# Token ring, squares' sums, held-back scores and the softmax's order in a fused attention and feed-forward kernel

## The chip, the cores and the metric

The kernel runs on one core of one Trainium2 chip. The metric is the device time of one execution in microseconds (us). Five engines work side by side, each with a queue of its own that it goes through in order: TensorE (PE in the profile, with its weight loads as PEld), VectorE (DVE), ScalarE (ACT), GpSimd (POOL) and SyncE (SP), which issues the transfers (DMA). They wait for one another by semaphores.

## What is computed

q, k and v are 6016 x 256. Attention goes over channels: the scores are a 256 x 256 matrix, summed over all tokens, of columns divided by their norms. Two feed-forward layers follow, with weights of 256 x 2048 and 2048 x 256 each.

```python
qn = q / (np.linalg.norm(q, axis=1, keepdims=True) + 1e-06)
kn = k / (np.linalg.norm(k, axis=1, keepdims=True) + 1e-06)
s = kn.transpose(0, 2, 1) @ qn / tau
s = s - s.max(-1, keepdims=True)
a = np.exp(s)
a /= a.sum(-1, keepdims=True) + 1e-09
x = v @ a
h = x @ w_in1;  x = (h * np.clip(h + 3.0, 0.0, 6.0) / 6.0) @ w_out1
h = x @ w_in2;  x = np.maximum(h, 0.0) ** 2 @ w_out2
```

## The kernel before

The whole program is written in one hand-made order (`manual_schedule`): the order of the calls in the code is the order on each engine's queue.

**Scores.** The tokens come in NT = 47 tiles of 128, q and k side by side, 256 KB a tile. GROUPS says how many tiles one transfer carries: one, then 23 times two. The transfers go through SP's queue into a ring of eight buffers (the tags wo0 to wo7); a transfer waits until TensorE has read the buffer's former tiles. For each tile ScalarE squares its 512 columns into a PSUM bank (`squares`, sq), VectorE adds the squares to one of two sums (`sums[t % 2]`), and TensorE adds to both halves of the scores (`score`: `s_ps[0]`, in the order's rows s_113, and `s_ps[1]`, s_114), each a float32 matmul of two passes. Of the last DEFER = 10 tiles the second half is held back (`late`). Ahead of the first tile come six fillers, matmuls on ones (`keep_busy`) that compute nothing.

**w_in1.** The weights arrive as 64-bit floats in units of 512 KB, which ScalarE and VectorE turn into pairs of float32r numbers, high and low, in several steps (`unit`, `from_float64`). Unit 0 is asked for with group 12 and converted while the scores run. Unit 1 (raw11l) is asked for behind the last group of q and k and converted behind the last tile.

**Softmax.** The norms' sums over the partitions are 8 matmuls with ones (`nrm`), one for each of the two sums and four blocks of columns. Then six of the held-back scores run while VectorE and ScalarE take the root, polish it and invert it. `rq_ps` spreads the inverse norms of q over the partitions; ScalarE copies it (L428). For each half, VectorE multiplies scores by both norms (L435), takes the row maximum (L439), and ScalarE takes the exponential (L442). TensorE transposes the result (`et_ps`), ScalarE and VectorE cut it into high and low parts (eth, etl). Fillers stand between.

**M and the first feed-forward layer.** M = et x w_in1 (256 x 2048) takes the place of v @ a @ w_in1. Its quarters c4 = 0 to 3 are made in two banks each (`mps`: mp_0, mp_1), which ScalarE and VectorE turn into weights (`m1_out`: wa_0h, wa_0l, a_0); `m1_keep` copies both banks to SBUF (m_01) for sums of M's blocks, which GpSimd and others make later. Then the steps of the loop run: a product of v's first 1024 tokens with M's blocks (h_n_f, `product` and `whole_product`), relu on ScalarE (`relu0`, L661), the gate on VectorE (`gate0`, L666), the cut into high (ScalarE, gs) and low (VectorE), and the accumulation with w_out1 (`second_both`, acc_0_n_d, LAG = 2 products behind). M's next quarter comes behind the product h_0_3.

## Time and profile before

| | us |
|---|---|
| median of 3 runs | 1039.83 |
| lowest and highest | 1038.69, 1040.44 |
| the profiled execution | 1040.8 |
| its span | 1039.0 |
| TensorE busy in the span | 1031.2 (99%) |
| VectorE, ScalarE, GpSimd busy | 855.5, 664.2, 30.9 |

The span runs from the first to the last instruction that the profile shows. Its stages are: start and scores up to 42 us, softmax up to 55.6 us, M's first quarter and the first steps up to 73.8 us, then the two feed-forward layers. A busy share says nothing on who waits for whom; for that one reads the stage, the idle time in front of an instruction, and what ended it.

### The profile page before, as it was taken

To read this page: it belongs to the slowest core of one execution; us is meant where nothing else is said; L and a number is where in the kernel's file an instruction comes from. 1 tells how busy PE (TensorE), PEld (TensorE's weight loads), DVE (VectorE), ACT (ScalarE), POOL (GpSimd) and SP (SyncE) were. 2 spreads that over 40 slices of the span, in tenths; PEclk is the share of its full clock that TensorE was granted. 3 is DMA by queue.
4 is the path that set the end of the run, shared out by engine and by line. 5 is a ranking of instruction groups with operands and counts; after the bars stand their busy time and mean duration, and the time that the engine had idled before them with its cause. 6 is when DMAs were issued, how large, how long until landed. Compare 5 with 4: busy or idle time off the path is not lost.

```text
span 1039.0 us, 12962 instructions
## 1 busy us (share of the span) xinstructions
PE 1031.2 (99%) x4630; PEld 867.5 (83%) x4630; DVE 855.5 (82%) x1429; ACT 664.2 (64%) x1200; POOL 30.9 (3%) x33
## 2 busy tenths in 40 slices
PE   9999999999999999999999999999999999999998
PEld 8878888888888888888998888888888888888997
DVE  6889978889989889888988688688688688778765
ACT  6788877788787878878766455445445455445443
POOL 0012240000000000000000000000000000000000
PEclk9999999999999999999999999999999999999999
DMA  9911203003403403302755002002001000200100
GB/s 363 355 29 53 83 14 130 1 1 130 145 1 116 157 1 117 131 23 103 261 184 188 1 1 81 0 1 81 1 1 47 36 1 6 71 1 1 41 1 36
DMA packets 25936, 77.64 MB, mean 75 GB/s; under 512 B 2832, under 2 KB 4880, under 8 KB 25872
## 3 DMA queue, kind: packets, MB, share of 16 engines
q1 hardware_dynamic: 25872, 76.82, 21.1%
q8 instruction: 36, 0.59, 0.2%
q14 instruction: 28, 0.23, 0.1%
HBM read 52.95 MB, written 23.86 MB: 74 GB/s over the span
## 4 chain that ended last, share of the span: by engine, by line
PE 96%; DVE 1%; ACT 1%; DMA 1%; issue 0%; SPq 0%
PE acc L323 15%; PE acc L322 15%; PE acc L321 15%; PE y L322 8%; PE y L323 8%; PE y L321 8%; PE q L323 4%; PE q L321 4%; PE q L322 4%; PE acc L689 4%; PE h L311 3%; PE s L300 3%; PE x L323 2%; PE x L321 2%; PE x L322 2%; PE mp L311 1%
## 5 line engine op out<-in xcount | busy, mean ns | idle before, releaser
L126 DVE TENSOR_TENSOR gs<-g,gs 128x512 fp32r<-128x512 f32 (+1 forms) x384 | 263.9, 687 | 60.2 <-ACT gs L841 48.1
L323 PE MATMUL acc<-gs,wo 128*128 128x512 f32 (+1 forms) x708 | 273.0, 386 | 0.1
L322 PE MATMUL acc<-gs,wo 128*128 128x512 f32 (+1 forms) x708 | 272.9, 385 | 0.0
L321 PE MATMUL acc<-gs,wo 128*128 128x512 f32 (+1 forms) x708 | 272.9, 385 | 0.0
L841 ACT CAST gs<-g 128x512 fp32r<-128x512 f32 (+1 forms) x352 | 208.1, 613 | 27.5 <-DVE g L832 18.9
L323 PEld LDWEIGHTS acc<-gs,wo 128*128 128x128 f32 x708 | 133.0, 188 | 25.2 <-DVE gs L126 0.5
L322 PEld LDWEIGHTS acc<-gs,wo 128*128 128x128 f32 x708 | 133.0, 188 | 24.8
L321 PEld LDWEIGHTS acc<-gs,wo 128*128 128x128 f32 x708 | 133.0, 188 | 24.4
L814 ACT COPY se<-y 128x512 f32<-128x512 f32 (+1 forms) x88 | 50.8, 577 | 124.1 <-PE y L323 124.0
L818 DVE TENSOR_TENSOR h<-q,se 128x512 f32<-128x512 f32 (+1 forms) x88 | 59.7, 678 | 65.5 <-ACT se L814 65.0
L814 ACT COPY su<-y 128x512 f32<-128x512 f32 (+1 forms) x88 | 50.8, 577 | 87.7 <-PE y L323 76.7
L837 DVE SCALAR_TENSOR_TENSOR g<-h 128x512 f32<-128x512 f32 (+1 forms) x144 | 97.1, 675 | 0.0
L824 ACT ACTIVATE r<-h,three 128x512 f32<-128x512 f32 (+1 forms) x120 | 85.6, 713 | 7.8 <-DVE h L818 7.5
L832 DVE SCALAR_TENSOR_TENSOR g<-r,h 128x512 f32<-128x512 f32 (+1 forms) x120 | 80.9, 674 | 3.9 <-ACT r L824 3.8
L826 ACT ACTIVATE r<-y 128x512 f32<-128x512 f32 (+1 forms) x48 | 28.3, 590 | 62.5 <-PE y L323 62.5
L818 DVE TENSOR_TENSOR h<-q,su 128x512 f32<-128x512 f32 (+1 forms) x88 | 59.5, 676 | 1.5
L818 DVE TENSOR_TENSOR h<-x,sa 128x512 f32<-128x512 f32 (+1 forms) x88 | 59.3, 674 | 0.0
L814 ACT COPY sa<-y 128x512 f32<-128x512 f32 (+1 forms) x88 | 50.7, 576 | 7.5 <-PE y L323 1.5
L837 DVE SCALAR_TENSOR_TENSOR g<-y,r 128x512 f32<-128x512 f32 (+1 forms) x48 | 32.7, 681 | 23.3 <-ACT r L826 22.7
L689 PE MATMUL acc<-gs,wo 128*128 128x512 f32 x180 | 45.3, 391 | 0.0
L300 PE MATMUL s<-qk 128*128 128x256 f32 x188 | 42.2, 385 | 0.9 <-DMA qk<-in_qk 0.9
L300 PEld LDWEIGHTS s<-qk 128*128 128x128 f32 x188 | 36.2, 194 | 6.1 <-DMA qk<-in_qk 1.3
(247 smaller groups left out, 1802.2 us busy)
## 6 DMA issues: line engine op xcount, KB each, us to landing
qk<-in_qk SPq DMA_DIRECT2D x23, 512.0 KB, 7.2
wo<-in_w_out SPq DMA_DIRECT2D x16, 512.0 KB, 5.6
wi<-in_w_in SPq DMA_DIRECT2D x10, 512.0 KB, 5.5
...
```

The lines of the kernel that those rows point to most:

```text
L126: eng.tensor_tensor(out=lo, in0=x, in1=f32(hi), op=ALU.subtract)
L300: nc.tensor.matmul(s_ps[i], lhsT=x[:, C + i * P:C + (i + 1) * P], rhs=x[:, :C], start=(t == 0), stop=(t == NT - 1))
L321: nc.tensor.matmul(ps, lhsT=ah, rhs=bh, start=first, stop=False, skip_group_check=more)
L322: nc.tensor.matmul(ps, lhsT=al, rhs=bh, start=False, stop=False, skip_group_check=more)
L323: nc.tensor.matmul(ps, lhsT=ah, rhs=bl, start=False, stop=last, skip_group_check=more)
L689: nc.tensor.matmul(acc[0, 0, n, d], lhsT=wo1[u][:, i, at + d * P:at + (d + 1) * P], rhs=gs[k], start=f == 0 and (i, k) == (0, 0), stop=f = ...
L814: nc.scalar.copy(s[tag], s["y"])
L818: nc.vector.tensor_tensor(out=s[which], in0=s[ps], in1=s[tag], op=ALU.add)
L824: nc.scalar.activation(s["r" + which], h, AF.Relu, bias=three)
L832: nc.vector.scalar_tensor_tensor(out=g, in0=s["r" + which], scalar=6.0, in1=h, op0=ALU.min, op1=ALU.mult)
L837: nc.vector.scalar_tensor_tensor(out=g, in0=h, scalar=0.0, in1=r, op0=ALU.max, op1=ALU.mult)
L841: nc.scalar.copy(gs[which][0], s["g" + which])
```

## The change

- *Transfers.* The first five tiles come one by one. The ring has twelve buffers, four of them (b4 to b7) the converter's tags. Units 0 and 1 of w_in1 are asked for with groups 8 and 14 and converted inside the loop, one step behind each of twelve tiles (CONVERT). tau's transfer moves from group 20 to group 10.
- *Sums.* There are three. The first tile of each is squared right into its sum, so the memsets go. Ten tiles (BY_POOL) go to the third, whose nine adds GpSimd makes from a square in SBUF; behind tile 42 VectorE adds it to the second. The later tiles all go to the first. The norms of the second sum are taken ahead of the last tile but one's scores, those of the first behind the last tile.
- *Scores held back.* 14, of which 6, 3 and 5 are issued (LATE).
- *Softmax.* The table of the exponential is loaded behind the root. One instruction, `tensor_tensor_reduce`, multiplies and takes the maximum; a small one negates it. The first half reads `rq_ps` in place; ScalarE has multiplied its scores by k's norms. The fillers of this stage go (seven), and there are seven at the start.
- *M and the first steps.* mp_0 and mp_1 are each made in one run (`m1_first`). The tokens' high parts are cut ahead of the second half's softmax. The first two products are made high parts first (`first_products`). h_1_0 and h_1_1 lie in the accumulators' banks. `m1_keep` copies mp_0 in step 1 and mp_1 in step 2 instead of ahead of the first product.

```diff
-GROUPS = [1] + [2] * 23
-DEFER = 10
-LATE_AT = 6
+GROUPS = [1] * 5 + [2] * 21
+RING = ("b4", "b5", "wo0", "wo1", "wo2", "wo3", "b6", "b7", "wo4", "wo5", "wo6", "wo7")
+DEFER = 14
+LATE = (6, 3, 5)
...
-BUSY = (6, 2, 2, 3)
+BUSY = 7
...
-EARLY = 12
-TAU_AT = 20
-EARLY_AT = {15: (0, 1), 16: (2,), 18: (3, 4)}
+EARLY = {8: 0, 14: 1}
+TAU_AT = 10
+CONVERT = {
+    15: (0, 0), 16: (0, 1), 17: (0, 2), 18: (0, 3), 19: (0, 4, 0), 20: (0, 4, 1),
+    27: (1, 0), 28: (1, 1), 29: (1, 2), 30: (1, 3), 31: (1, 4, 0), 32: (1, 4, 1),
+}
+BY_POOL = (4, 7, 10, 13, 22, 24, 26, 33, 35, 37)
+JOIN_AT = 42
+FIRST_SUM_AT = 45
...
     def squares(t, x):
-        sq = bank([P, 2 * C], f"sq{t}")
+        at, eng = (2, nc.gpsimd) if t in BY_POOL else (0 if t > JOIN_AT else t % 2, nc.vector)
+        if at not in begun:
+            begun.add(at)
+            nc.scalar.activation(sums[at], x, AF.Square)
+            return
+        if at == 2:
+            sq = hpool.tile([P, 2 * C], F32, tag="r", name=f"sq{t}")
+        else:
+            sq = bank([P, 2 * C], f"sq{t}")
         nc.scalar.activation(sq, x, AF.Square)
-        nc.vector.tensor_tensor(out=sums[t % 2], in0=sq, in1=sums[t % 2], op=ALU.add)
+        eng.tensor_tensor(out=sums[at], in0=sq, in1=sums[at], op=ALU.add)
...
+                if t == JOIN_AT:
+                    nc.vector.tensor_tensor(out=sums[1], in0=sums[1], in1=sums[2], op=ALU.add)
+                if t == FIRST_SUM_AT:
+                    nrm = ps_acc.tile([P, 8], F32, tag="acc", name="nrm")
+                    norms(4, 1)
                 score(t, x, 0)
...
+        norms(0, 0)
+        late_scores(LATE[0])
+        first = small(4)
+        nc.vector.tensor_copy(first, nrm[:, 4:8])
...
+        late_scores(LATE[1])
+        s0k = small(C)
+        nc.scalar.activation(s0k, s_ps[0], AF.Copy, scale=rnorm[:, 2:3])
...
-            nc.vector.scalar_tensor_tensor(
-                out=s, in0=s_ps[i], scalar=rnorm[:, 2 + i:3 + i], in1=rq, op0=ALU.mult, op1=ALU.mult
+            mx, low = small(1), small(1)
+            a, b, scale = (s0k, rq_ps, 1.0) if i == 0 else (s_ps[1], rq, rnorm[:, 3:4])
+            nc.vector.tensor_tensor_reduce(
+                out=s, in0=a, in1=b, scale=scale, scalar=-3.0e38, op0=ALU.mult, op1=ALU.max, accum_out=mx
             )
-            mx = small(1)
-            nc.vector.tensor_reduce(out=mx, in_=s, axis=AX.X, op=ALU.max, negate=True)
+            nc.vector.tensor_scalar(out=low, in0=mx, scalar1=-1.0, scalar2=None, op0=ALU.mult)
...
+        e0 = softmax(0)
+        nc.scalar.copy(rq, rq_ps)
+        loaded[0][2]()
+        loaded[0][3]()
+        transposed(0, *e0)
+        rest(0, *e0)
+        row_sums(0, *e0)
+        late_scores(LATE[2])
+        for k in range(KC):
             for n in range(2):
...
+                first_tokens(k, n, 0)
+        for n in range(2):
+            first_tokens(0, n, 1)
         e1 = softmax(1)
...
+        m1_first(0)
+        transposed(1, *e1)
+        row_sums(1, *e1)
+        for n in range(2):
+            first_tokens(1, n, 1)
+        rest(1, *e1)
+        m1_high(0, 0)
+        m1_first(1)
+        m1_low(0, 0)
+        m1_high(0, 1)
+        m1_low(0, 1)
...
-        m1_keep(0)
...
+                if at in (2, 3):
+                    hs[at] = ps_acc.tile([P, WMAX], F32, tag="acc", name=name)[:, :w0]
+                else:
+                    hs[at] = bank([P, WMAX], name)[:, :w0]
...
+            if a in (1, 2):
+                m1_keep(0, (a - 1,))
```

SP's queue near the end of the tokens, before (raw11l is unit 1 of w_in1, v the first tokens of v):

```order
L338 DMA qk_379<-in_qk 128x1024 [waits DMAHW5_49,PE_49,Activation_49]
L346 DMA tau_sb<-in_tau 128x1 [waits DMAHW6_49]
L338 DMA qk_392<-in_qk 128x1024 [waits DMAHW7_49,PE_49,Activation_49]
L338 DMA qk_402<-in_qk 128x1024 [waits DMAHW0_49,PE_49,Activation_49]
L338 DMA qk_412<-in_qk 128x1024 [waits DMAHW1_49,PE_49,Activation_49]
L184 DMA raw11l<-in_w_in 128x1024 [waits DMAHW2_49]
L380 DMA v_0_425<-in_vt 128x1024 [waits DMAHW3_49]
L380 DMA v_1_426<-in_vt 128x1024 [waits DMAHW4_49]
```

And now, with the last group of tokens at the second piece's head:

```order
L361 DMA qk_285<-in_qk 128x1024 [waits DMAHW0_49,PE_49,Activation_49]
L191 DMA raw11l<-in_w_in 128x1024 [waits DMAHW1_49]
L361 DMA qk_298<-in_qk 128x1024 [waits DMAHW2_49,PE_49,Activation_49]
...
L361 DMA qk_407<-in_qk 128x1024 [waits DMAHW3_49,PE_49,Activation_49]
L361 DMA qk_417<-in_qk 128x1024 [waits DMAHW4_49,PE_49,Activation_49]
L201 DMA wo_0_434<-in_w_out 128x1024 [waits DMAHW5_49]
L409 DMA v_0_436<-in_vt 128x1024 [waits DMAHW6_49]
```

Unit 1 has moved from behind all tokens to a place with eleven groups behind it, tau's transfer has left this stretch, and a unit of w_out1 stands ahead of v.

TensorE's queue from the norms to the first half of M, before (busy are fillers):

```order
L396 MATMUL nrm<-both,scratch_109 128x1 x7
L300 MATMUL s_114<-qk_369 128x256 x2
L300 MATMUL s_114<-qk_379 128x256 x2
L300 MATMUL s_114<-qk_392 128x256 x2
L421 MATMUL rq_ps<-scratch_110,both 128x128 [waits DVE_49] x2
L300 MATMUL s_114<-qk_402 128x256 x2
L300 MATMUL s_114<-qk_412 128x256 x2
L286 MATMUL busy_487<-both 128x128 x2
L448 MATMUL et_ps_486<-both,scratch_111 128x128 [waits PE_49,Activation_49,Pool_49]
L448 MATMUL et_ps_486<-both,scratch_111 128x128
L286 MATMUL busy_507<-both 128x128 x2
L321 MATMUL mp_0_510<-wi1h_355,eth 128x512 [waits Activation_49]
```

And now:

```order
L354 MATMUL nrm<-both,scratch_109 128x1 x3
L314 MATMUL s_114<-qk_356 128x256 x2
L314 MATMUL s_114<-qk_366 128x256 x2
L314 MATMUL s_114<-qk_376 128x256 x2
L446 MATMUL rq_ps<-scratch_110,both 128x128 [waits DVE_49] x2
L314 MATMUL s_114<-qk_386 128x256 x2
L314 MATMUL s_114<-qk_396 128x256
L473 MATMUL et_ps_480<-both,scratch_111 128x128 [waits PE_49,Activation_49,Pool_49]
L473 MATMUL et_ps_480<-both,scratch_111 128x128
L314 MATMUL s_114<-qk_396 128x256
L314 MATMUL s_114<-qk_407 128x256 x2
L314 MATMUL s_114<-qk_417 128x256 x2
```

Only the first sum's norms are left here, the transposes stand between three and five held-back scores, and the fillers are gone.

ScalarE's queue ahead of the first relu, and around the third gate's cast (gs_1_0), before:

```order
L495 ACTIVATE wa_0h<-mp_1_547,rs_518 128x2x256 [waits DVE_49,PE_49]
L511 ACTIVATE m_01_556<-mp_0_510,rs_504 128x512 [waits DVE_49]
L511 ACTIVATE m_01_556<-mp_1_547,rs_518 128x512 [waits DVE_49]
L158 ACTIVATE tywi_2_538<-raw12h 128x512 [waits Activation_49]
L661 ACTIVATE r_0_0_586<-h_0_0_572,three 128x512 [waits PE_49,Pool_49]
L661 ACTIVATE r_0_1_588<-h_0_1_576,three 128x512 [waits PE_49]
...
L158 ACTIVATE tywi_3_626<-raw12l 128x512
L124 CAST gs_1_0_639<-g_1_0_637 128x512 [waits DVE_49]
L661 ACTIVATE r_0_2_664<-h_0_2_657,three 128x512 [waits PE_49,Activation_49]
```

And now:

```order
L519 ACTIVATE wa_0h<-mp_1_531,rs_520 128x2x256 [waits DVE_49,PE_49]
L131 CAST wo_0_542<-tawo_0_471 128x512
L162 ACTIVATE tbwi_2_547<-raw12h 128x512 [waits DMAHW0_49]
L165 ACTIVATE tywi_2_548<-raw12h 128x512
L697 ACTIVATE r_0_0_573<-h_0_0_559,three 128x512 [waits PE_49,Pool_49]
L697 ACTIVATE r_0_1_575<-h_0_1_560,three 128x512 [waits PE_49,Pool_49]
...
L131 CAST gs_0_1_606<-g_0_1_604 128x512 [waits DVE_49]
L535 ACTIVATE m_01_610<-mp_0_510,rs_488 128x512
...
L131 CAST gs_1_0_628<-g_1_0_626 128x512 [waits DVE_49]
L535 ACTIVATE m_01_610<-mp_1_531,rs_520 128x512
```

The copies of mp_0 and mp_1 (m_01) stand behind the casts of the second and the third gate.

TensorE's queue around the product h_1_2, before:

```order
L689 MATMUL acc_0_0_0_648<-gs_0_1_619,wo_0_499 128x512 [waits DVE_49]
L689 MATMUL acc_0_0_1_649<-gs_0_1_619,wo_0_499 128x512
L311 MATMUL h_1_2_681<-x_0_3_527,wa_0h 128x512 x2
L311 MATMUL h_1_2_681<-x_0_5_533,wa_0h 128x512 x2
L311 MATMUL h_1_2_681<-x_0_3_527,wa_0l 128x512
L311 MATMUL h_1_2_681<-x_0_5_533,wa_0l 128x512
L689 MATMUL acc_0_1_0_695<-gs_1_0_639,wo_0_499 128x512 [waits Activation_49]
L689 MATMUL acc_0_1_0_695<-gs_1_0_639,wo_0_499 128x512
```

And now:

```order
L725 MATMUL acc_0_0_0_638<-gs_0_1_606,wo_0_542 128x512 [waits DVE_49]
L725 MATMUL acc_0_0_1_639<-gs_0_1_606,wo_0_542 128x512
L325 MATMUL h_1_2_671<-x_0_3_498,wa_0h 128x512 [waits Activation_49]
L325 MATMUL h_1_2_671<-x_0_3_498,wa_0h 128x512
L325 MATMUL h_1_2_671<-x_0_5_502,wa_0h 128x512 x2
L325 MATMUL h_1_2_671<-x_0_3_498,wa_0l 128x512
L325 MATMUL h_1_2_671<-x_0_5_502,wa_0l 128x512
L725 MATMUL acc_0_1_0_685<-gs_1_0_628,wo_0_542 128x512 [waits DVE_49]
L725 MATMUL acc_0_1_0_685<-gs_1_0_628,wo_0_542 128x512
L725 MATMUL acc_0_1_1_686<-gs_1_0_628,wo_0_542 128x512 [waits DVE_49]
```

h_1_2 now waits for ScalarE, and the accumulators of n = 1 wait for VectorE twice.

## Rows read from the trace of the kernel before

**Rows 1.** Stages: us, busy PE, PEld, DVE, ACT, POOL, clock, DMA share, GB/s.

```profile
8.28:42.05 33.77, 33.77 (x156) 29.80 (x157) 30.02 (x50) 26.84 (x49) 0.55 (x1) 1.00 1.00 376
42.05:55.59 13.54, 12.45 (x71) 10.24 (x69) 10.66 (x29) 9.16 (x21) 0.00 (x0) 1.00 0.71 289
55.59:73.81 18.22, 17.71 (x73) 13.51 (x74) 16.04 (x27) 14.42 (x25) 3.43 (x4) 1.00 0.10 29
73.81:1031.80 957.99, 957.86 (x4294) 806.10 (x4294) 793.47 (x1318) 608.92 (x1099) 25.96 (x19) 1.00 0.18 60
```

**Rows 2.** TensorE's timeline, start: start us, us, operation, [idle before, releaser].

```profile
1.13 2.93 PE L286 MATMUL busy<-both 128*128 128x128 f32 x12 [1.13 <-POOL both L113]
3.85 3.57 PE L300 MATMUL s<-qk 128*128 128x256 f32 x12
8.28 0.92 PE L300 MATMUL s<-qk 128*128 128x256 f32 x3 [0.86 <-DMA qk<-in_qk]
```

**Rows 3.** ScalarE's timeline at the start.

```profile
9.62 4.81 ACT L296 ACTIVATE sq<-qk 128x512 f32<-128x512 f32 x8 [0.18 <-DMA qk<-in_qk]
```

**Rows 4.** The squares' tile: ns least/median/most, first and last start.

```profile
L296 ACT ACTIVATE sq<-qk x47: 573/583/602, 3.5 to 39.0; 128x512 f32<-128x512 f32 x47
L297 DVE TENSOR_TENSOR scratch<-sq,scratch x47: 680/683/694, 4.1 to 40.6; 128x512 f32<-128x512 f32 x47
```

**Rows 5.** TensorE's timeline: the norms' sums and the norms' product.

```profile
42.05 1.84 PE L396 MATMUL nrm<-both,scratch 128*128 128x1 f32 x16
...
46.43 0.61 PE L421 MATMUL rq_ps<-scratch,both 128*128 128x128 f32 x4
```

**Rows 6.** VectorE's timeline: the softmax's first half.

```profile
47.79 0.49 DVE L435 SCALAR_TENSOR_TENSOR scratch<-s,scratch 128x256 f32<-128x256 f32 x1 [0.91 <-ACT scratch L428]
48.31 0.42 DVE L439 TENSOR_REDUCE scratch<-scratch 128x1 f32<-128x256 f32 x1
...
52.13 0.15 DVE L456 TENSOR_SCALAR rs<-scratch 128x1 f32<-128x1 f32 x1
```

**Rows 7.** ScalarE's timeline: exponential in two parts, cast behind the transposes.

```profile
48.77 0.51 ACT L442 ACTIVATE scratch<-scratch 128x256 f32<-128x256 f32 x1 [1.01 <-DVE scratch L439]
49.18 0.19 ACT L442 ACTIVATION_READ_ACCUMULATOR scratch<-scratch 128x1 f32 x1
49.92 0.37 ACT L449 CAST eth<-et_ps 128x256 fp32r<-128x256 f32 x1 [0.55 <-PE et_ps L448]
```

**Rows 8.** TensorE's timeline: first product, h_1_2, and accumulations around M's next quarter.

```profile
55.59 0.50 PE L321 MATMUL h<-x,wa_0h 128*128 128x512 f32 x1 [0.49 <-ACT wa_0h L495]
...
66.06 1.09 PE L311 MATMUL h<-x,wa_0h 128*128 128x512 f32 x4
...
67.64 1.65 PE L689 MATMUL acc<-gs,wo 128*128 128x512 f32 x6
...
73.65 1.53 PE L689 MATMUL acc<-gs,wo 128*128 128x512 f32 x6
```

**Rows 9.** VectorE's timeline: the first gate, its neighbours, and L167 later, alone.

```profile
59.39 0.69 DVE L666 SCALAR_TENSOR_TENSOR g<-r,h 128x512 f32<-128x512 f32 x1 [0.86 <-ACT r L661]
59.99 1.20 DVE L167 CUSTOM_DVE_ANT_0 tawi<-tawi,tywi 128x1024 uint16<-128x1024 uint16 x1
61.11 1.22 DVE L126 TENSOR_TENSOR gs<-g,gs 128x512 fp32r<-128x512 f32 x1
...
69.43 0.69 DVE L167 CUSTOM_DVE_ANT_0 tawi<-tawi,tywi 128x1024 uint16<-128x1024 uint16 x1
```

**Rows 10.** ScalarE's timeline: both copies of M's quadrants, the third gate's cast.

```profile
56.84 1.35 ACT L511 ACTIVATE m<-mp,rs 128x512 f32<-128x512 f32 x2 [0.37 <-DVE a L499]
...
66.98 0.61 ACT L124 CAST gs<-g 128x512 fp32r<-128x512 f32 x1
```

**Rows 11.** GpSimd: timeline beside the first gates; an add's group (us, mean ns).

```profile
60.60 1.19 POOL L216 TENSOR_TENSOR m<-m,m 128x256 f32<-128x256 f32 x1
...
L772 POOL TENSOR_TENSOR x<-raw,x 128x512 fp32r<-128x512 f32 x5 | 6.8, 1365 | 17.7 <-PE h L311 13.4 <-ACT x L768 4.3
```

More of the change, by code (lines that the diff above doesn't have):

```diff
@@ L335, in attention_then_two_ffns, with norms @@
         t = 0
+        def norms(at, m):
+            for b in range(4):
+                nc.tensor.matmul(
+                    nrm[:, at + b:at + b + 1], lhsT=sums[m][:, b * P:(b + 1) * P], rhs=ones[:, 0:1],
+                    start=True, stop=True,
+                )
         for gi, n in enumerate(GROUPS):
-            src = wpool.tile([P, 1024], F32, tag=f"wo{gi % NU}", name=f"qk{gi}")[:, :2 * n * C]
+            src = wpool.tile([P, 1024], F32, tag=RING[gi % len(RING)], name=f"qk{gi}")[:, :2 * n * C]
             nc.sync.dma_start(
@@ L380, in load_x, with late_scores @@
                 nc.sync.dma_start(out=raw[k][:, :, :w], in_=(vt[p] if j == 0 else x2_d[p])[:, 2 * k:2 * k + 2, :w])
-        pre.append(unit("wi1", 1, raw1[1]))
+        feed()
         raw0 = [gpool.tile([P, 2, WMAX], F32, tag="g", name=f"v0_{k}") for k in range(KC)]
         load_x(0, 0, raw0)
-        for _ in range(AHEAD):
+        for _ in range(AHEAD - 1):
             feed()
-        for st in range(4):
-            pre[1][st]()
-        nrm = ps_acc.tile([P, 4], F32, tag="acc", name="nrm")
-        for b in range(4):
-            for m, x in enumerate(sums):
-                nc.tensor.matmul(
-                    nrm[:, b:b + 1], lhsT=x[:, b * P:(b + 1) * P], rhs=ones[:, 0:1], start=(m == 0), stop=(m == 1)
-                )
-        for a in late[:LATE_AT]:
-            score(*a)
+        held_back = iter(late)
+        def late_scores(n):
+            for _ in range(n):
+                score(*next(held_back))
+        norms(0, 0)
+        late_scores(LATE[0])
+        first = small(4)
+        nc.vector.tensor_copy(first, nrm[:, 4:8])
         x2n = small(4)
-        nc.vector.tensor_scalar_max(x2n, nrm, 1e-30)
+        nc.vector.scalar_tensor_tensor(out=x2n, in0=nrm[:, :4], scalar=1e-30, in1=first, op0=ALU.max, op1=ALU.add)
         root = small(4)
         nc.scalar.activation(root, x2n, AF.Sqrt, scale=2.0 ** -10)
-        pre[1][4](0)
+        nc.scalar.activation(warm, ones[:, 0:1], AF.Exp)
         rec = small(4)
@@ L505, in m1_out, with m1_keep @@
             m1_low(c4, k)
-        def m1_keep(c4):
-            for k in range(KC):
+        def m1_keep(c4, ks=range(KC)):
+            for k in ks:
                 if k == 0:
@@ L640, in weight0, with first_products @@
             return [t[:, u, (A12, A22)[odd] if k else A11, :] for t in wa1[c4]]
-        def product(at, k):
-            if at < len(steps):
+        def first_products():
+            for at in range(2):
                 n, f = steps[at]
-                if k == 0:
-                    hs[at] = bank([P, WMAX], f"h0_{n}_{f}")[:, :w0]
-                passes(hs[at], [(weight0(f, k), x0[k, n])], k == 0, k == KC - 1)
+                hs[at] = bank([P, WMAX], f"h0_{n}_{f}")[:, :w0]
+            for k in range(KC):
+                for part in ((0, 0), (0, 1)), ((1, 0),):
+                    for at in range(2):
+                        n, f = steps[at]
+                        for a, b in part:
+                            nc.tensor.matmul(
+                                hs[at], lhsT=weight0(f, k)[a], rhs=x0[k, n][b],
+                                start=k == 0 and (a, b) == (0, 0), stop=k == KC - 1 and a == 1,
+                            )
         def whole_product(at):
@@ L942, in attention_then_two_ffns @@
             at(last - (NU - 2 - 2 * c4) * SLOTS + 0.1, lambda c4=c4: load_wa2(c4))
-        for kk in range(KC):
-            for a in range(2):
-                product(a, kk)
+        first_products()
         relu0(0)
```

76 lines of the change are left out of this document (25 added, 51 removed).

## The prediction

> **What bounds the kernel now.** I read the busy time of each engine by stage first [rows 1]. From 73.81 us to the last microseconds TensorE works 957.86 of 957.99 us: nothing but its own matmuls sets the time there, and the change leaves that stretch's instructions and their order as they are. So the question is only how much sooner TensorE comes to the accumulation that starts at 73.65 us [rows 8]. Call that moment M. In front of it lie three stages. The scores (8.28 to 42.05 us) keep TensorE busy all the time, but DMA too has a busy share of 1.00. The softmax stage (42.05 to 55.59 us) has TensorE busy for 12.45 of 13.54 us, part of that with passes on ones that compute nothing; its length is set by a chain through ScalarE and VectorE. The third stage (to 73.81 us) has TensorE busy for 17.71 of 18.22 us.
>
> Then I read the seams. The start: three fillers, then scores that wait for the second 512 KB [rows 2]; ScalarE waits for tokens too [rows 3]. The scores' end: the last square starts at 39.0 us [rows 4], and the norm sums on TensorE end at 42.05 + 1.84 = 43.89 us [rows 5]. Call that end T. After it I read the softmax on VectorE and ScalarE [rows 6, 7], and the first products and gates [rows 8 to 10].
>
> The sum is made against the profiled execution: 1040.8 us, of which 1039.0 are its span. The median of three is 1039.83 us, 0.97 less; the difference that I work out is taken off the median.
>
> **The change part by part.**
>
> *Start.* Five 256 KB pieces in place of one and two 512 KB ones let a tile's scores start when its own half has landed. The gap that this can fill is 0.86 us [rows 2]. One more filler here is two passes of 2.93 / 12 = 0.24 us. I take a gain of 0.5 us, with 0.1 and 0.9 as bounds. It gives TensorE slack only; whether the end of the stage sees it is decided by the tokens, below.
>
> *Scores.* A score matmul is two passes. 156 passes took 33.77 us [rows 1], so one score is 0.433 us. From the sixth tile, which I put at 9.6 us (ScalarE's tokens are there at 9.62 [rows 3]), 28 tiles with both halves, 14 with one and 16 norm passes of 1.84 / 16 = 0.115 us [rows 5] are 24.2 + 6.1 + 1.8 = 32.1 us: TensorE by itself would end the norms at 41.7 us. Four more scores held back (4 x 0.433 = 1.73 us) are moved, not saved.
>
> *Tokens and sums.* The 512 KB of the second w_in1 unit stood behind all q and k; now it stands in front of the last eleven groups, on SP's one queue. From 8.28 us, when TensorE's wait for the second group ended [rows 2], to 9.62, when ScalarE's for the third did [rows 3], are 1.34 us for 512 KB. Twelve buffers let the transfers be issued earlier, but DMA's share was 1.00 already [rows 1], so I take the whole 1.34 us (bounds 0 and 1.34). The last square then starts at 39.0 + 1.3 = 40.3 us, ends 0.58 us later, its add (0.683 us [rows 4]) is done at 41.6, and eight norm passes (the other eight, for the second sum, now run earlier) end at 41.6 + 0.9. So **T' = 42.5 us**, 1.4 us sooner than before, with TensorE waiting about 0.8 us in front of the last norms. The start's half microsecond and the larger ring are hidden by this.
>
> *GpSimd's squares.* Nine adds on GpSimd at 1.365 us (the nearest rows with that shape and operands in SBUF [rows 11]) are 12.3 us, spread over 34 tiles: off the path. VectorE loses twelve adds, 12 x 0.683 = 8.2 us. That is not a gain by itself, since VectorE was busy for 30.02 of 33.77 us [rows 1] and followed the tokens; it makes room for the conversions of the second unit.
>
> The bound against it is sharing: next to a GpSimd instruction two VectorE instructions took 1.20 and 1.22 us [rows 9], where the same one took 0.69 alone. Nine such losses would be 9 x 0.51 = 4.6 us, less than the 8.2 us that leave. So I take 0. The Trainium skill ("SBUF — State Buffer", Who interferes with whom) says that a VectorE instruction with two inputs in SBUF contends with a GpSimd instruction that reads SBUF, and one with at most one such input doesn't. The squares' adds read one input from PSUM, so by this rule the adds would lose nothing; the trace has no square's add next to GpSimd, and the sum stands at 0 by both.
>
> *Softmax stage, counted from T'.* Up to the norms' product the chain is as before: its four passes end at 46.43 + 0.61 = T + 3.15 us [rows 5]; six scores (2.6 us) cover it. Before, ScalarE then copied that product, so VectorE started at 47.79 and the exponential at 48.77, T + 4.88 [rows 6, 7]. Now VectorE reads it in place. The new instruction that multiplies and takes the maximum in one is in no row: I bound it, with the negation, by 0.49 + 0.15 = 0.64 us and 0.49 + 0.42 + 0.15 = 1.06 [rows 6], and take 0.85. The exponential starts at T' + 4.05, its two parts end 0.70 us later [rows 7]. The transposes run at T' + 4.75, after three of eight scores; the remaining five last to T' + 7.3. So TensorE waits some 0.4 us where it ran fillers.
>
> In front of the second half's multiply VectorE does the first low half (0.42), the row sums (0.15 + 0.16) and two token rests of about 0.62: it begins at T' + 7.65 and ends at 8.5; the exponential ends at 9.2; the transposes and the cast (0.37 [rows 7]) at about 10.0. The second half's six passes take until T' + 11.4, the casts of M's high parts on ScalarE (0.69 each) come with them, and the twelve passes of the first products, with their waits for low halves, end near T' + 14.4. The first gate on VectorE starts at **T' + 15.1**. Before it was 59.39 = T + 15.50 [rows 9]. So the reordered softmax, with 1.73 us more scores and less filler in it, is worth 0.4 us beyond T.
>
> *Third stage.* Two copies of M's quadrants (1.35 us for both [rows 10]) stood in front of the first relu; now they stand behind the casts of the second and the third gate. ScalarE's queue is where it counts: from the first relu to the second copy lie 15 instructions. Before, first gate to the end of the third cast was 66.98 + 0.61 - 59.39 = 8.2 us [rows 9, 10]. GpSimd's work, which started behind those copies and slowed two VectorE instructions by 0.51 and 0.53 us [rows 9, 11], moves on: minus 1.04 if all of it is gone (bounds 0 and 1.04). The copies add 1.35. So the second copy ends at T' + 15.1 + 8.2 - 1.04 + 1.35 = T' + 23.6.
>
> Who waits for it is the matmul group h_1_2: its bank is the second of M's, freed by that copy. Behind it on TensorE's queue stand the accumulations of the third gate. Before, h_1_2 ran from 66.06 us, ahead of that gate's cast, and the accumulation began at 67.64, just as the cast ended [rows 8, 10]; now it starts behind the cast. TensorE is ready for it at T' + 14.4 + 2.7 (two products) + 1.4 + 1.4 + 1.4 = T' + 21.3. **A new wait of 2.3 us** thus takes back most of what the stage ahead won. After it come, at 0.227 us a pass [rows 8], h_1_2 (1.36), an accumulation (1.46), h_0_3 (1.46) and M's next two products (2.72): M' = T' + 30.7 = 42.5 + 30.7 = 73.2 us. Against 73.65 that is 0.4 us sooner: 1039.83 - 0.4 = **1039.4 us**.
>
> **The rivals.**
>
> *Tokens in time.* If the deeper ring brings the last tokens as early as before (38.4 us), T' is TensorE's 41.7, M' = 72.4 and the time 1038.6. For it: the transfers were issued one by one behind TensorE. Against it: DMA's share of 1.00. Chance 0.20.
>
> *The new wait is hidden.* ScalarE idled in the third stage (14.42 of 18.22 us busy [rows 1]), so the two copies may fill idle time; with the chain 1.4 to 2.3 us shorter, TensorE's queue decides: M' = T' + 28.4 to 29.3, with T' between 41.7 and 42.5, and the time 1036.7 to 1038.0; I put it at 1037.5. Against it: 15 instructions of about 0.6 us on ScalarE are 9 us by themselves. Chance 0.22.
>
> *The clock falls: slower than before.* Seven fillers are gone from the softmax stage, and TensorE would stand still for 0.8 us ahead of the norms, twice about half a microsecond in the softmax, and 2.3 us ahead of h_1_2. At the start the fillers' passes came at 0.24 us each, against 0.61 us for four of that form later, their latency included [rows 2, 5]: the lower of the two levels (1.2 and 2.4 GHz). I estimate that it lasted from 1.13 to about 5.5 us, since the first twelve score passes took 3.57 us [rows 2] where 12 x 0.216 = 2.6 would do. In 4.4 us half of the work, 2.2 us, is lost. One such fall gives 1039.4 + 2.2 = 1041.6 us; from 5 us at the lower level on, the loss passes 0.2%. For: the wait ahead of h_1_2 is longer than any that the trace shows after the start. Against: the granted clock reads 1.00 in each stage, and after the wait of 0.86 us at 7.4 us the passes went on at full speed. The Trainium skill ("TensorE: Matmul & The Clock Gate", Part 1: The HAM clock gate) says that the clock is a gate, set by how busy the array has been of late, and that idling brings the lower level back. By that rule dropping the fillers is a risk; the trace shows no fall at all. Chance 0.10.
>
> **How the numbers follow.** Forecast 0.48 (1039.4), tokens in time 0.20 (1038.6), wait hidden 0.22 (1037.5), clock 0.10 (1041.6). The range leaves 2 in 10 out: the lower end takes in most of the hidden wait, 1037.0; the upper end the forecast with its costs at their worse bounds (no contention saved 1.0, the multiply 0.2 twice), 1039.4 + 1.4 = 1040.8, and a little of the last case: 1041.0. About 0.2% (2.1 us) is what a measurement of this kernel can tell from no change, so faster means below 1037.75, and slower above 1041.9. Faster: 0.15 of the hidden wait, 0.05 of tokens in time, 0.04 of the forecast's spread: 0.24. Slower: 0.05 of the clock and 0.03 of a chain that is longer than I think: 0.08. The same: 0.68.
>
> **What would show it.** The last norms should end near 42.5 us, behind a wait for VectorE (41.7 without); the last square start near 40.3; the first exponential 4.05 us after the norms; the first gate 15.1 us after them; h_1_2 wait some 2 us for ScalarE's copy of M; the accumulation after M's next products start at 73.2 us, with 958 us behind it. I'd be wrong if TensorE's passes near 60 us double, if squares' adds next to GpSimd take well over 0.68 us, or if h_1_2 doesn't wait.

## The result, and the profile after

The changed kernel takes 1045.56 us (median of 6 runs, 1042.81 to 1048.38) against 1039.61 for the kernel before in the same session: a ratio of 1.0056, with a 95% interval of 1.0041 to 1.0070. It is slower, by 4 to 7 us. The prediction said 1039.4 us, between 1037.0 and 1041.0, and gave slower a chance of 0.08. Its numbers are wrong; the case that came is one of its rivals, the clock, and on top of it the sums were late.

The stages of the changed kernel, cut where TensorE starts or stops to wait; columns as in [rows 1]:

```profile
9.37:39.15 29.78, 29.78 (x136) 25.70 (x136) 21.78 (x35) 23.70 (x44) 12.29 (x11) 1.00 1.02 412
39.15:41.22 2.07, 0.00 (x2) 0.00 (x1) 2.07 (x5) 2.07 (x5) 0.00 (x0) 1.00 1.02 416
41.22:52.00 10.78, 10.78 (x36) 9.08 (x37) 4.63 (x14) 3.54 (x7) 0.00 (x0) 0.53 0.69 263
52.00:69.95 17.95, 17.22 (x76) 13.11 (x74) 15.09 (x34) 13.69 (x29) 0.00 (x0) 1.00 0.13 40
69.95:72.19 2.24, 0.00 (x1) 0.00 (x0) 1.85 (x4) 2.24 (x6) 0.00 (x0) 1.00 0.05 22
72.19:75.60 3.41, 3.41 (x9) 2.68 (x10) 3.33 (x6) 2.39 (x4) 3.30 (x3) 0.55 0.00 0
...
80.75:1038.00 957.25, 957.25 (x4293) 805.54 (x4291) 791.54 (x1315) 607.45 (x1096) 25.57 (x19) 1.00 0.18 60
```

Twice TensorE stands still for more than 2 us, and twice the granted clock then reads 0.53 and 0.55: the lower of its levels, 1.2 GHz, in nearly all of the stretch. The first fall lasts some 10 us, the second about 3. From 80.75 us on the kernel is the old one, 957 us at full clock. TensorE's timeline names the waits:

```profile
41.22 1.36 PE L354 MATMUL nrm<-both,scratch 128*128 128x1 f32 x8 [2.07 <-DVE scratch L377]
...
44.29 1.79 PE L354 MATMUL nrm<-both,scratch 128*128 128x1 f32 x8
45.94 5.47 PE L314 MATMUL s<-qk 128*128 128x256 f32 x12
51.20 1.01 PE L446 MATMUL rq_ps<-scratch,both 128*128 128x128 f32 x4
...
72.19 1.82 PE L325 MATMUL h<-x,wa_0h 128*128 128x512 f32 x4 [2.24 <-ACT m L535]
...
80.75 1.52 PE L725 MATMUL acc<-gs,wo 128*128 128x512 f32 x6
```

The first wait is for the join of GpSimd's sum (L377), the second, ahead of h_1_2, for the copy of M's second bank. Behind the first, twelve passes of held-back scores take 5.47 us; before, they took 2.84 at full clock:

```profile
43.76 2.84 PE L300 MATMUL s<-qk 128*128 128x256 f32 x12
```

T' is 44.29 + 1.79 = 46.08 us (before 43.89 [rows 5]), M' 80.75 (before 73.65 [rows 8]): M' is 7.1 us later in this execution, which is the longest of the six (1048.38 us). Roughly, the six times follow the mean clock over the span: 0.998 with 1042.8 and 1044.1 us, 0.996 with 1045.5, 1045.7 and 1046.6, 0.993 with 1048.4.

Why the join was late is read on the engines that feed it. First the squares' tile, as in [rows 4], then ScalarE and VectorE near the end of the tokens:

```profile
L310 ACT ACTIVATE sq<-qk x44: 573/586/632, 6.1 to 41.0; 128x512 f32<-128x512 f32 x44
L311 DVE TENSOR_TENSOR scratch<-sq,scratch x35: 678/691/693, 6.7 to 43.5; 128x512 f32<-128x512 f32 x35
L311 POOL TENSOR_TENSOR scratch<-sq,scratch x9: 1269/1275/1758, 11.3 to 37.7; 128x512 f32<-128x512 f32 x9
```

```profile
32.73 0.62 ACT L131 CAST wi1h<-tawi 128x512 fp32r<-128x512 f32 x1 [1.51 <-DVE tawi L174]
...
36.33 5.28 ACT L310 ACTIVATE sq<-qk 128x512 f32<-128x512 f32 x10 [0.41 <-POOL scratch L311]
```

```profile
37.49 3.08 DVE L311 TENSOR_TENSOR scratch<-sq,scratch 128x512 f32<-128x512 f32 x5 [0.84 <-ACT sq L310]
40.48 0.68 DVE L377 TENSOR_TENSOR scratch<-scratch,scratch 128x512 f32<-128x512 f32 x1
41.09 3.08 DVE L311 TENSOR_TENSOR scratch<-sq,scratch 128x512 f32<-128x512 f32 x4
```

ScalarE stood still for 1.51 us in front of the cast of w_in1's unit 1, because VectorE had not finished its part of the conversion, and for 0.41 us because GpSimd had not read a square; its squares then ran back to back to 41.6 us. VectorE got the last squares late, had the join in its queue, and its last four adds, all into one sum, took 3.08 us, as long as the five alternating ones ahead of them. The last add ends near 44.2 us.

### The profile page after: what moved, and what is told of

Read it like the earlier page. It is cut to its first block, busy times and chain, and to the rows that moved or that the text cites. A ratio compares the mean times of both kernels' runs of the same rounds, so it can differ in the third digit from the quotient of the medians.

```text
span 1046.6 us, 12918 instructions
## 1 busy us (share of the span) xinstructions
PE 1035.3 (99%) x4618; PEld 869.9 (83%) x4618; DVE 848.3 (81%) x1419; ACT 664.4 (63%) x1201; POOL 43.4 (4%) x42
## 4 chain that ended last, share of the span: by engine, by line
PE 94%; DMA 2%; ACT 2%; DVE 1%; issue 1%; SPq 0%; POOL 0%; ACTq 0%; POOLq 0%
PE acc L337 15%; PE acc L336 15%; PE acc L335 15%; PE y L336 7%; PE y L337 7%; PE y L335 7%; PE q L337 4%; PE q L335 4%; PE q L336 4%; PE acc L725 4%; PE h L325 4%; PE x L337 2%; PE x L335 2%; PE x L336 2%; DMA qk<-in_qk 2%; PE mp L325 1%
## 5 line engine op out<-in xcount | busy, mean ns | idle before, releaser
L133 DVE TENSOR_TENSOR gs<-g,gs 128x512 fp32r<-128x512 f32 (+1 forms) x384 | 263.3, 686 | 61.6 <-ACT gs L877 48.0
L314 PE MATMUL s<-qk 128*128 128x256 f32 x188 | 45.8, 404 | 0.4 <-DMA qk<-in_qk 0.4
```

The costliest lines, as they stand in the source:

```text
L133: eng.tensor_tensor(out=lo, in0=x, in1=f32(hi), op=ALU.subtract)
L314: nc.tensor.matmul(s_ps[i], lhsT=x[:, C + i * P:C + (i + 1) * P], rhs=x[:, :C], start=(t == 0), stop=(t == NT - 1))
```

## The experiments

The theory at the start. **A:** the clock's falls cost most of the loss. **B:** the waits and longer chains cost it, whatever the clock does. Then, on the sums, **D1:** ScalarE's wait for the conversion makes them late; **D2:** GpSimd does.

### Fillers in the waits

Matmuls on ones where TensorE stood still; no wait is taken away. In three kernels: at all places, ahead of h_1_2 alone, around the norms alone.

```diff
+                    fill(10, nrm[:, P:])
                     norms(4, 1)
...
+        fill(6, nrm[:, P:])
         norms(0, 0)
...
+            if a == 4:
+                fill(10, bank([P, P], "busy_h", tag="x"))
             if a:
                 whole_product(a + 1)
```

> The changed kernel with fillers (matmuls on ones) put where TensorE stood still in its trace: ten ahead of the second sum's norms (a wait of 2.07 us), six ahead of the first sum's norms, ten ahead of h_1_2 (2.24 us). No wait is taken away. Theory A, the clock: two falls to the lower level, 42 to 52 us and 72 to 75.6 us in the changed kernel's trace, cost most of the loss. Then the clock stays at 1.00 through both places, the last norms end near 45.1 us (the sum's last add ends at 44.2), the accumulation behind M's next products starts near 75.5 us (80.75 in the changed kernel, 73.65 before), and the time is 1041.4 us (1040.6 to 1042.2). Theory B, the waits alone: the chains are longer whatever the clock does; then the time stays at 1045.6 us (1044.5 to 1046.5).

> The changed kernel with ten fillers ahead of h_1_2 alone. Theory A: the second fall (72 to 75.6 us, 1.7 us of work lost) goes, the first stays: the accumulation behind M's next products 1.7 us sooner than without, counted from the last norms (33.0 us in place of 34.7), and the time 1043.9 us (1043.0 to 1044.8). Theory B: no change, 1045.6 us.

> The changed kernel with the sixteen fillers around the norms alone, none ahead of h_1_2. Theory A: the first fall goes, the second stays in most runs (clock 0.998 to 0.999). With fillers at all three places the time was 1042.0, with those ahead of h_1_2 alone 1044.8, without any 1045.6: the two prices add if this one is near 1042.7 us (1041.8 to 1043.6).

Measured, each against the kernel before in its own session: 1041.99 us with all of them against 1038.88 (9 runs, ratio 1.0027, 1.0017 to 1.0037), 1044.84 with those ahead of h_1_2 alone against 1038.88 (5 runs, 1.0052, 1.0039 to 1.0065), 1041.94 with those around the norms alone against 1039.12 (7 runs, 1.0032, 1.0020 to 1.0043). All at once, by stage, with the first exponential, the first gate and M':

```profile
39.34:45.83 6.49, 6.49 (x54) 6.24 (x53) 4.98 (x8) 2.74 (x6) 0.14 (x1) 1.00 1.03 417
...
66.55:69.00 2.45, 2.42 (x22) 2.23 (x20) 2.06 (x5) 2.45 (x6) 0.00 (x1) 1.00 0.07 27
```

```profile
49.77 0.51 ACT L473 ACTIVATE scratch<-scratch,scratch 128x256 f32<-128x256 f32 x1 [0.29 <-DVE scratch L470]
```

```profile
60.48 0.69 DVE L708 SCALAR_TENSOR_TENSOR g<-r,h 128x512 f32<-128x512 f32 x1
```

```profile
75.93 1.52 PE L731 MATMUL acc<-gs,wo 128*128 128x512 f32 x6
```

Work that computes nothing makes the kernel faster: by 3.0 us when the ratios to the kernel before are compared (1.0056 less 1.0027; the intervals don't meet). The plain medians differ by 3.6, but the kernel before was 0.7 us faster in that session too. The clock reads 1.00 through both places, and the runs lie within 1.7 us of each other (5.6 without). That shows A: the falls cost time, and 1041.99 lies in A's range. But by the ratios they are about half of the loss, not most of it. What is left, 2.8 us above the kernel before, is B's: sums and chain at full clock.

Within the noise the prices add, and nearly all lies at the norms: by ratios the fillers there bring 2.5 us, those ahead of h_1_2 0.4, all together 3.0. The 0.4 alone can't be told from nothing. With fillers around the norms alone TensorE stood still ahead of h_1_2 for as long as before, and the clock held:

```profile
68.55 1.19 PE L329 MATMUL h<-x,wa_0h 128*128 128x512 f32 x4 [2.26 <-ACT m L541]
...
75.48 1.52 PE L731 MATMUL acc<-gs,wo 128*128 128x512 f32 x6
```

```profile
68.00:70.00 2.00, 1.45 (x6) 1.24 (x7) 2.00 (x4) 1.21 (x3) 1.35 (x2) 1.00 0.00 0
```

So a wait of 2.26 us is followed by a fall in one execution and not in another; two of this kernel's seven runs had a mean clock of 0.997 and 0.998. In the kernel with fillers ahead of h_1_2 alone the first wait (1.99 us) and fall remained and the second fall was gone: M' - T' is 32.57 us in its profile, where the changed kernel's has 34.67. Its time, 1044.84, lies at the edge between the two theories' numbers and decides nothing.

### The copies of M's banks

First both copies in step 1; then the third stage as before, both copies ahead of the first relu and h_1_0 and h_1_1 in ordinary banks.

```diff
-            if a in (1, 2):
-                m1_keep(0, (a - 1,))
+            if a == 1:
+                m1_keep(0)
```

```diff
+        m1_keep(0)
         for part in range(2):
             loaded[0][4](part)
...
-                if at in (2, 3):
-                    hs[at] = ps_acc.tile([P, WMAX], F32, tag="acc", name=name)[:, :w0]
-                else:
-                    hs[at] = bank([P, WMAX], name)[:, :w0]
+                hs[at] = bank([P, WMAX], name)[:, :w0]
...
-            if a in (1, 2):
-                m1_keep(0, (a - 1,))
```

> The changed kernel with both copies of M's banks made in step 1, so that the second stands ahead of the third gate's cast. h_1_2 should not wait for it any more; the third gate's cast comes 0.6 us later. Theory A: the wait of 2.24 us and the fall of the clock behind it (1.7 us) both go, less the 0.6: 1045.6 - 3.3 = 1042.3 us (1041.5 to 1043.5). Theory C, the wait only moves to the accumulation of the third gate: about 0.6 us better, 1045.0 us, and the clock falls there.

> The changed kernel with the third stage as before: both copies of M's banks ahead of the first relu, and h_1_0 and h_1_1 in the banks of M instead of the accumulators'. Theory A: the wait ahead of h_1_2 (2.24 us) and the second fall behind it (1.7 us) go, the copies cost up to 1.35 us ahead of the first relu and the sharing with GpSimd up to 1.04; the first fall stays. 1045.6 - 2.2 = 1043.4 us (1042.3 to 1044.4), the clock at 1.00 from 54 us on. Rival: the wait turns up in front of another instruction and the time stays at 1045 to 1046 us.

Measured: 1046.88 us (5 runs, ratio 1.0070, 1.0056 to 1.0084) and 1045.31 (5 runs, 1.0055, 1.0043 to 1.0067); theory A's numbers (1042.3 and 1043.4) fell. C's 1045.0 for the first was missed too: that kernel is no faster than the changed one. The second lies where its rival put it. With both copies in step 1, on TensorE and VectorE:

```profile
72.06 0.73 PE L725 MATMUL acc<-gs,wo 128*128 128x512 f32 x2 [0.88 <-ACT gs L131]
74.89 1.86 PE L725 MATMUL acc<-gs,wo 128*128 128x512 f32 x4 [2.09 <-DVE g L702]
```

```profile
70.97 1.17 DVE L133 TENSOR_TENSOR wo<-tawo,wo 128x512 fp32r<-128x512 f32 x1 [0.93 <-ACT wo L131]
...
74.16 0.67 DVE L702 SCALAR_TENSOR_TENSOR g<-r,h 128x512 f32<-128x512 f32 x1
```

h_1_2 no longer waits, but the accumulators of n = 1 do: for the third gate's cast, and then for the fourth gate, since h_1_1 lies in the second accumulator's bank. In the changed kernel the accumulators depend on the same gate, hidden behind the longer wait. The clock fell here as well (0.50 from 76 to 78 us). With the third stage as before:

```profile
67.63 1.66 PE L723 MATMUL acc<-gs,wo 128*128 128x512 f32 x6 [1.47 <-ACT gs L131]
```

```profile
62.83 0.61 ACT L131 CAST wo<-tawo 128x512 fp32r<-128x512 f32 x1
63.34 0.67 ACT L162 ACTIVATE tbwi<-raw12h 128x512 f32<-128x512 f32 x1
63.91 0.66 ACT L165 ACTIVATE tywi<-raw12h 128x512 int32<-128x512 uint32 x1
64.47 1.25 ACT L695 ACTIVATE r<-h,three 128x512 f32<-128x512 f32 x2
```

The wait moved to the first accumulation: the change has also put a cast and two conversion steps (1.6 us) between M's copies and the first relu, where before one such step stood. Here the clock read 1.00 from 52 us on, so the second fall was gone, and the time stayed all the same. Each of the two kernels traded a wait for another.

### The sums

Unit 1's cast three tiles later; no squares on GpSimd.

```diff
-    27: (1, 0), 28: (1, 1), 29: (1, 2), 30: (1, 3), 31: (1, 4, 0), 32: (1, 4, 1),
+    27: (1, 0), 28: (1, 1), 29: (1, 2), 30: (1, 3), 34: (1, 4, 0), 35: (1, 4, 1),
```

```diff
-BY_POOL = (4, 7, 10, 13, 22, 24, 26, 33, 35, 37)
+BY_POOL = ()
...
-                if t == JOIN_AT:
+                if t == JOIN_AT and BY_POOL:
```

> The changed kernel with the last two steps of unit 1's conversion (the cast and its rest) at tiles 34 and 35 in place of 31 and 32. In the changed kernel ScalarE stood still for 1.51 us in front of that cast, with all later squares behind it. Theory D1, that wait is what makes the sums late: the wait ahead of the second sum's norms falls from 2.07 to under 0.8 us, the first sum's last add ends near 42.7 (44.2), the clock holds until the norms, and the time is 1040.5 to 1042.5 us. Theory D2, GpSimd's adds and the join hold the sums: the wait and the time stay within 0.7 us of the changed kernel's 1045.6.

> The changed kernel with no squares on GpSimd: VectorE adds all of them into two sums, and there is no join. Theory D1 (ScalarE's wait for VectorE's part of the conversion): VectorE has nine more adds (6.1 us) and falls behind further, the sums end at 44 to 46 us and the time is 1045 to 1047.5 us. Theory D2 (GpSimd's slow adds are the cause): the sums end near 42 us, and the time is 1041 to 1043 us.

Measured: 1044.39 us (6 runs, ratio 1.0044, 1.0031 to 1.0057) and 1045.01 (5 runs, 1.0050, 1.0037 to 1.0062). With the later cast, TensorE and VectorE:

```profile
40.15 1.05 PE L354 MATMUL nrm<-both,scratch 128*128 128x1 f32 x8 [1.28 <-DVE scratch L377]
```

```profile
34.47 1.24 DVE L133 TENSOR_TENSOR wi1l<-tawi,wi1h 128x512 fp32r<-128x512 f32 x1
...
40.01 3.08 DVE L311 TENSOR_TENSOR scratch<-sq,scratch 128x512 f32<-128x512 f32 x4
```

The wait shrank from 2.07 to 1.28 us and the last add ended 1.1 us sooner, so the cast's wait is part of the cause, as D1 says; but the last four adds still took 3.08 us, and the clock fell all the same, after 1.28 us and another wait of 0.97. The later place had a price of its own: the conversion's last step on VectorE (L133) now ran beside GpSimd's adds and took 1.24 us in place of 0.68. D1's time (1040.5 to 1042.5) was wrong. Without GpSimd's squares VectorE had no pause:

```profile
35.86 8.64 DVE L311 TENSOR_TENSOR scratch<-sq,scratch 128x512 f32<-128x512 f32 x13
```

The last add ends at 44.5 us, as in the changed kernel. D2 falls, and the sums' end and the time are where D1 put them: GpSimd's squares neither cost nor gain much. At the end VectorE's queue is the limit in both kernels: it runs without a pause from 35.86 us on here, and from 37.49 us on in the changed kernel.

### The kernel before without its softmax fillers

```diff
-BUSY = (6, 2, 2, 3)
+BUSY = (6, 0, 0, 0)
```

> The kernel before without its seven fillers in the softmax stage; nothing else is changed. They took 14 passes, about 1.5 us, in time in which TensorE would wait. Theory A1, these fillers hold the clock up: it falls in the softmax stage and the time is 1041.5 to 1044.5 us. Theory A2, only the two longer waits of the changed kernel let it fall: the granted clock stays 1.00 and the time is 1039.6 us, within 0.5.

Measured: 1039.54 us (11 runs) against 1038.88, ratio 1.0006 (0.9997 to 1.0015): no difference that can be told. Yet the clock fell, in nearly every run (mean 0.998 in ten of eleven):

```profile
48.00:50.00 2.00, 0.83 (x5) 0.33 (x3) 1.97 (x5) 1.15 (x4) 0.00 (x0) 1.00 1.04 424
...
52.00:54.00 2.00, 2.00 (x6) 1.52 (x6) 1.56 (x6) 1.99 (x5) 0.00 (x0) 0.50 0.03 8
```

TensorE was busy for 0.83 of 2 us, with single waits of 0.7 us and less, and ran at half clock from 51 to 55 us. M lies at 73.52 us all the same. I take it that ScalarE and VectorE set the pace in that stretch; this is argued from M, not tested. A fall costs what TensorE's passes then hold up, and here that was little. Both theories had a part wrong: A1 the time, A2 the clock.

### Setting right what was found

Four kernels, each built on the one ahead. The first: third stage as before, unit 1's cast at tile 34, GpSimd's last tiles at 29, 32 and 35, join at tile 39, late tiles alternating, both sums' norms behind the last tile.

```diff
-JOIN_AT = 42
+JOIN_AT = 39
...
-        at, eng = (2, nc.gpsimd) if t in BY_POOL else (0 if t > JOIN_AT else t % 2, nc.vector)
+        at, eng = (2, nc.gpsimd) if t in BY_POOL else (t % 2, nc.vector)
...
+        late_scores(2)
+        norms(4, 1)
         norms(0, 0)
```

> Several parts set right at once: the third stage as before; unit 1's cast at tile 34; GpSimd's last tiles at 29, 32 and 35 and the join behind tile 39; the late tiles alternate between the two sums; both sums' norms behind the last tile, with two held-back scores ahead of them and three fewer behind the first transposes. Theory A with D1: no wait of TensorE over 1 us until 55 us, the clock at 1.00, the last norms end at 42.0 to 43.0 us, the accumulation behind M's next products starts at 71.5 to 72.5 (73.65 before), and the time is 1.0 to 2.2 us below the kernel before, 1037 to 1038.5 us. Rival: a wait or a fall of the clock remains, and the time is 1040 to 1042 us.

Measured: 1042.83 us (5 runs, ratio 1.0034, 1.0022 to 1.0046); the profiled run 1041.48 at a clock of 1.000, the other four at 0.997 and 0.998. Its waits on TensorE, and VectorE beside GpSimd:

```profile
41.62 1.95 PE L354 MATMUL nrm<-both,scratch 128*128 128x1 f32 x16 [1.59 <-DVE scratch L311]
...
61.81 1.66 PE L723 MATMUL acc<-gs,wo 128*128 128x512 f32 x6 [1.46 <-ACT gs L131]
...
73.80 1.53 PE L723 MATMUL acc<-gs,wo 128*128 128x512 f32 x6
```

```profile
30.36 1.17 DVE L174 CUSTOM_DVE_ANT_0 tawi<-tawi,tywi 128x1024 uint16<-128x1024 uint16 x1
31.45 2.07 DVE L311 TENSOR_TENSOR scratch<-sq,scratch 128x512 f32<-128x512 f32 x3
...
33.44 1.34 DVE L133 TENSOR_TENSOR wi1l<-tawi,wi1h 128x512 fp32r<-128x512 f32 x1
```

The adds end 2 us sooner than in the changed kernel, but two conversions beside GpSimd's adds took 1.17 and 1.34 us in place of 0.69. M' is 73.80, level with the kernel before, while three parts were taken back. Neither the theory (1037 to 1038.5) nor its rival (1040 to 1042) has the median. The second kernel moves unit 1's conversion to tiles 24 to 31 away from eight GpSimd tiles, puts three held-back scores and four fillers ahead of the norms, and makes the first two products in the old order:

> The last kernel with four more changes: unit 1's conversion at tiles 24 to 31; GpSimd's squares (eight tiles) kept away from VectorE's conversions, since there two VectorE instructions with both inputs in SBUF took 1.17 and 1.34 us beside GpSimd in place of 0.68; three held-back scores and four fillers ahead of the norms; the first two products in the order of the kernel before, so that the first of them ends three passes sooner. Theory A with D: VectorE's last add ends near 41 us (42.2), the last norms near 42.0 to 42.5, no wait of TensorE over 1 us and the clock at 1.00 in all runs (so the median is the profiled run's time within 0.5 us), the accumulation behind M's next products at 71.6 to 72.6 (73.80 in the last kernel, 73.65 before), and the time 1037 to 1038.5 us. Rival: the first gate's chain through ScalarE and VectorE sets the end whatever TensorE does ahead of it, and the time is 1039 to 1041 us.

Measured: 1042.11 us (8 runs, ratio 1.0029, 1.0019 to 1.0040), M' at 75.11: outside both ranges, with the rival (1039 to 1041) nearer. The ring of four banks for squares held ScalarE for 1.22 us behind VectorE, which now has more of the late adds, and the first relu stood behind ScalarE's other work:

```profile
40.47 1.20 ACT L314 ACTIVATE sq<-qk 128x512 f32<-128x512 f32 x2 [1.22 <-DVE scratch L315]
```

The third gives GpSimd two more late tiles, moves a cast and a conversion step on ScalarE into its wait for M's second bank, and adds five fillers:

```diff
         m1_high(0, 0)
+        loaded[0][4](0)
+        feed()
+        loaded[1][0]()
         m1_first(1)
```

> The last kernel, with GpSimd's tiles at 4, 7, 10, 13, 20, 22, 33, 35, 37 and 39 (two more late ones, so that VectorE has fewer late adds) and the join behind tile 43; with the cast of w_out1's first unit and one conversion step moved on ScalarE from behind M's copies, where they stood ahead of the first relu, into its wait for M's second bank (1.10 us idle in the last kernel's trace); and with five fillers ahead of the second transposes. Theory: the sums end near 41 us, the last norms at 42.0 to 43.0, the first relu starts within 0.3 us of the first product's end, the accumulation behind M's next products starts at 71.3 to 72.8 us (75.11 in the last kernel, 73.65 before), and the time is 1037 to 1038.5 us. Rival: the ring of four banks for squares ties ScalarE to VectorE, the sums end at 42 to 43.4 us all the same, and the time is 1039 to 1041 us.

Measured: 1040.78 us (11 runs, ratio 1.0016, 1.0007 to 1.0025), from 1038.93 at a clock of 1.000 to 1042.41 at 0.997. M' is 72.75 us, 0.9 sooner than in the trace before, yet that execution took 1039.20 us, level with the median of the kernel before in its session (1039.12). The rival's numbers came: VectorE's last add ended at 42.3 us, and the time lies in 1039 to 1041. Not its ring, though: from 30 us on ScalarE's squares waited for GpSimd (0.42 and 0.24 us), not for VectorE. Between M's copies and the first relu only one step is left in ScalarE's queue, where there were a cast and two:

```profile
57.09 0.66 ACT L165 ACTIVATE tywi<-raw12h 128x512 int32<-128x512 uint32 x1
57.65 1.26 ACT L697 ACTIVATE r<-h,three 128x512 f32<-128x512 f32 x2
```

The fourth has ten more fillers in the waits of 0.2 to 0.5 us that were left:

> The last tuned kernel (its times ran from 1038.9 at a mean clock of 1.000 to 1042.4 at 0.997) with fillers in the waits of 0.2 to 0.5 us that were left in the softmax stage: two ahead of the first transposes, two ahead of M's first bank, two more ahead of the second transposes, three ahead of M's second bank, one more ahead of the norms. Theory A: such short waits still decide in some executions whether the clock falls; then it holds at 1.000 in nearly all runs, and the median comes down to that kernel's undisturbed times, 1038.8 to 1039.8 us. Rival: the falls come from elsewhere, the clock still reads 0.997 to 0.998 in some of the runs, and the median stays at 1040.5 to 1041.5 us.

Measured: 1040.55 us (11 runs, ratio 1.0016, 1.0007 to 1.0025), clock 0.998 in three runs: the rival. Filling the short waits didn't hold the clock in every run; where it falls there, no profile of these runs shows. None of the kernels beats the one before.

## Why the prediction was wrong, point by point

**The sums (T').** The prediction put the last norms at 42.5 us. With the clock held they end at 45.83 (all fillers) and 45.45 (fillers around the norms), 3.0 to 3.3 us later, later even than before. The tokens were not the reason: they came at 412 GB/s where [rows 1] had 376, and TensorE had no wait for them from 9.37 us on. The step that failed is the term behind them, which has the last square start at 40.3 us and its add done at 41.6. It followed one tile through idle engines. The square started at 41.0, since ScalarE had lost 1.5 us to unit 1's cast; and the last add ended at 44.2, since VectorE's queue was full and its last four adds, into one sum, came at 0.79 us each where alternating ones come at 0.60. Of these 2.6 us the later cast took back 1.1, and alternating adds with other places for cast, join and GpSimd's tiles 2.0 (42.2); how much each of those parts is worth by itself is not shown. The sentence that the conversions had room on VectorE was an argument from busy time. It said nothing of ScalarE standing in its queue for VectorE, which is what happened.

**The clock.** The prediction had the mechanism, the places (the norms and h_1_2) and the sign, and gave it 0.10. Its evidence against, a wait of 0.86 us without a fall [rows 2], was the wrong yardstick for waits of 2 us that it itself forecast. Its price, 2.2 us for one fall, was taken from the kernel's start. There the passes came slowly, 0.24 us each (0.12 in the kernel with all fillers, where twenty passes took 2.40 us), but the granted clock of that stretch reads 1.00, so the lower level that the estimate stands on isn't shown:

```profile
1.13:5.50 4.37, 4.37 (x16) 4.07 (x17) 1.44 (x3) 2.09 (x4) 0.36 (x3) 1.00 0.78 262
```

Here the first fall lasted some 10 us, and removing both is worth 3.0 us by the fillers. By the Trainium skill ("TensorE: Matmul & The Clock Gate", Part 1: The HAM clock gate) the default is the throttled clock and activity releases it. The traces agree: the clock fell after TensorE had stood still (a wait of 2.07 us, then a granted clock of 0.53), though not after every such wait, and fillers kept it up. That rule spoke against this change and should have weighed more than a trace that had no such wait to show.

**Softmax stage.** Right, once the clock holds. The first exponential came at 49.77 - 45.83 = 3.94 us behind the norms (4.05 predicted), the first gate at 14.65 (15.1). The new instruction, in the changed kernel,

```profile
52.36 0.42 DVE L461 CUSTOM_DVE_ANT_0 scratch<-scratch,rq_ps 128x256 f32<-128x256 f32 x1 [3.75 <-PE rq_ps L446]
52.70 0.08 DVE L461 DVE_READ_ACCUMULATOR2_ANT scratch<- 128x1 f32 x1
52.82 0.15 DVE L464 TENSOR_SCALAR scratch<-scratch 128x1 f32<-128x1 f32 x1
```

takes 0.61 us with its read and the negation, where I took 0.85; the lower bound was 0.64. The exponential's two parts, put at 0.70 us, overlap: by [rows 7] they end 0.60 us behind its start.

**Third stage.** Right: a new wait of 2.3 us ahead of h_1_2 was predicted, 2.24 came, for the instruction named. M' - T' was to be 30.7 us and is 30.1 and 30.0 with the clock held. Before it was 73.65 - 43.89 = 29.8: nothing was won by it, as the sum said. (Its terms add up to 30.6, not 30.7, and the rival of the hidden wait reaches down to 1036.3 by its own bounds, not 1036.7; neither changes a reading.)

**GpSimd's squares.** Right in cost: 1.27 us each, off the path but for the 0.41 us that ScalarE waited for one. The adds beside them kept 0.69 us, and instructions with both inputs in SBUF took up to 1.34 (the first kernel set right). So the Trainium skill's rule ("SBUF — State Buffer", Who interferes with whom) agrees with these runs on both sides.

**The sum.** With the clock held the kernel lies 1.0027 to 1.0032 times the kernel before: 1042.6 to 1043.2 us on the prediction's base of 1039.83, 3.2 to 3.8 above the forecast and outside the range even so. M' holds 2.3 to 2.7 of that (75.48 and 75.93 where 73.2 was forecast): the sums' 3 us less 0.6 in the chain behind them. The rest stays open. The falls of the clock bring 2.5 to 3.0 more. Of the three signs of being wrong that the prediction named none came: TensorE's passes did double, but at 41 to 52 and 72 to 76 us and not near 60.

The forecast also took the stretch behind M' as fixed. From M' to the start of the output's last copy are 961.28 us in the trace before and 961.32 in the changed kernel's, but 960.15 and 960.08 in those with all fillers and with fillers around the norms. Of the fourteen traces six have the longer value and eight the shorter, at a granted clock of 1.00: from 500 to 540 us TensorE ran 195 or 196 matmuls in the ones and 199 in the others. What sets this is not shown. It puts 1.2 us between single executions whatever stands in front, so M' compares two traces better than their times do.
